# Chunked attention and a feed-forward layer on one core: head pairs scored in row tiles, later operands turned by the DMA crossbar, the front ordered by token tile

## The chip, the core and the metric

The kernel runs on one core of one Trainium2 chip. The metric is device time in microseconds (us), from the start to the end of one execution. The engines are TensorE (PE, matmuls), VectorE (DVE), ScalarE (ACT), GpSimd (POOL) and SyncE (SP, which only issues DMAs here). The kernel before was run three times.

## The reference

Four batches, eight heads, 768 positions, 64 numbers a head, all in float32. Attention is local: the positions go in chunks of 32, and the 32 queries of a chunk see eight memory keys, the chunk itself, 16 positions to its left and 8 to its right.

```python
for c in range(nc):                       # 24 chunks of 32
    k_full = concat(mem_k, k[l_start:r_end])   # 8 + up to 56 keys
    scores = q_c @ k_full.T / sqrt(64)
    a = softmax(scores)                   # 1e-9 is added to the sum
    out[c] = a @ concat(mem_v, v[l_start:r_end])
x = out as (4, 768, 512)
xn = (x - mean(x)) / sqrt(var(x) + 1e-6) * g
result = x + relu(xn @ w_ch1) @ w_ch2     # 512 -> 2048 -> 512
```

## The kernel before

**Tiles and units.** The 3072 tokens are 24 tiles of 128, six a batch. A tile holds two groups of 64 queries, so a batch has twelve groups. The feed-forward part works in units, a list called `units`: tiles 0 to 2 together, then tiles 3, 4 and 5 alone, then six units of three tiles. A unit runs 16 up steps (function `up`, L291: four matmuls each, of 128 columns for every tile of the unit; the ReLU goes to DVE at L299 and to ACT at L297 in turn) and then four down steps a tile (`down`, L308, four matmuls of 512 columns each, then the product with the root of the variance and the sum with x at L315, and the store from SP at L318).

**Attention of a tile** is four functions. `scores` (L212) does, per group and pair of heads, one matmul of 128x128 by 128 columns: the two heads of a pair lie in rows 0 to 63 and 64 to 127, and QZ, the query operand, holds zeros where a head meets the other's keys. Two exponentials on ACT (L219) follow, with a bias column that hides what a chunk must not see. `values` (L231) does 16 matmuls of 65 columns, of which the last column is the count of ones that gives the softmax's sum; DVE takes the reciprocal (L238), multiplies (L239), and takes statistics (L246, L247). The centred token is written at L258 (DVE) or L253 (POOL). `turn_x` (L274) turns it in four PE transposes and DVE copies it out (L279).

**Keys and queries** are loaded by POOL in runs of 512 numbers for a whole batch or two parts of it (`load_kq`), cast to fp16 on the way. `kq_block` turns them on PE (L188) and copies them to KT on DVE (L196) and QZ on ACT (L204). V is loaded in runs of 64 numbers (L106, L112); its left and right borders are copied from neighbour groups by SP (`v_before`, `v_after`), the memory values by `v_mem`.

**Order.** There is no scheduler: every engine runs its instructions in the order in which the Python code issues them. Work beside a unit is put into a dictionary, `plan`, which says after which step it is issued. In the first unit the plan has the scaling of w1 by the gain g (`scale_w1`, L154, 16 instructions on DVE), the clears of the second V buffer (`clear_v`, L334 to L336), its counts (L340) and the clears of KT and QZ (L346 to L349). [...] Two PSUM slots called `att` serve attention, four called `mm` serve the feed-forward part, each in turn.

Of the kernel before, what the change touches and what calls it, by code (L numbers as in the profile page):

```python
# [15 lines left out]
def kernel(  # L16
# [15 lines left out]
    FF = 2048  # L32
    NG = 12
    KR = 104
    BLK = 72
    KC = 24 + NG * BLK + 32
    HD = 65
    CUT = 64
# [6 lines left out]
    memk16 = sb.tile([8, B * H, 64], FP16, name="memk16")  # L45
    memv16 = sb.tile([8, B, H, HD], FP16, name="memv16")
    memKT = sb.tile([128, B * 4, 8], FP16, name="memKT")
    g_col = sb.tile([128, 4], FP32, name="g_col")
    band = sb.tile([128, 2], FP32, name="band")
    zero2 = sb.tile([128, 2], FP32, name="zero2")  # L50
    ones3 = sb.tile([128, 3], FP16, name="ones3")
    hole = sb.tile([128, 1], FP16, name="hole")
# [3 lines left out]
    k16 = [sb.tile([96, H, 8, 64], FP16, name=f"k16_{i}") for i in range(2)]  # L56
    q16 = [sb.tile([96, H, 8, 64], FP16, name=f"q16_{i}") for i in range(2)]
    V = [sb.tile([128, NG, H, HD], FP16, name=f"V{i}") for i in range(2)]
    KT = [sb.tile([128, 4, KC], FP16, name=f"KT{i}") for i in range(2)]
    QZ = [sb.tile([128, 4, NG, 2, 64], FP16, name=f"QZ{i}") for i in range(2)]  # L60
    AT = [sb.tile([128, 2, H, 64], FP16, name=f"AT{i}") for i in range(3)]
    xs = [sb.tile([128, 512], FP32, name=f"xs{i}") for i in range(9)]
    xn = [sb.tile([128, 512], FP16, name=f"xn{i}") for i in range(3)]
    xT = [sb.tile([128, 4, 384], FP16, name=f"xT{i}") for i in range(2)]
    rT = [sb.tile([128, 384], FP16, name=f"rT{hc}") for hc in range(16)]
# [3 lines left out]
    nmean = [sb.tile([128, 1], FP32, name=f"nmean{i}") for i in range(3)]  # L69
# [16 lines left out]
    def free(ap, off, pattern, parts=None):  # L86

        p = list(ap.ap[0]) if parts is None else [ap.ap[0][0], parts]
        return bass.AP(tensor=ap.tensor, offset=ap.offset + off, ap=[p] + [list(x) for x in pattern])
# [3 lines left out]


    HS = S * D

    def load_kq(b, which, lo=0, hi=96):

        dst, src = ((k16, k), (q16, q))[which]
        nc.gpsimd.dma_start(  # L100
            out=dst[b % 2][lo:hi, :, :, :],
            in_=dram(src, b * H * HS + 512 * lo, [[512, hi - lo], [HS, H], [1, 512]]),
        )

    def load_v_group(b, g):
        nc.gpsimd.dma_start(  # L106
            out=V[b % 2][24:88, g, :, 0:64],
            in_=dram(v, b * H * HS + 64 * g * D, [[64, 64], [HS, H], [1, 64]]),
        )

    def load_v_head(b, h):
        nc.gpsimd.dma_start(  # L112
            out=V[b % 2][24:88, :, h, 0:64],
            in_=dram(v, (b * H + h) * HS, [[64, 64], [64 * 64, NG], [1, 64]]),
        )

    def load_v_after(b, g):

        nc.gpsimd.dma_start(
            out=V[b % 2][96:104, g, :, 0:64],  # L120
            in_=dram(v, b * H * HS + 64 * (g + 1) * D, [[64, 8], [HS, H], [1, 64]]),
        )

    def v_before(b, g0, g1):
        vt = V[b % 2]
        nc.sync.dma_start(out=vt[0:16, g0:g1, :, :], in_=vt[72:88, g0 - 1 : g1 - 1, :, :])

    def v_after(b, g0, g1):
        vt = V[b % 2]
        nc.sync.dma_start(out=vt[96:104, g0:g1, :, :], in_=vt[24:32, g0 + 1 : g1 + 1, :, :])  # L130

    def v_mem(b):
        vt = V[b % 2]
        src = memv16[:, b, :, :]
        nc.sync.dma_start(
            out=vt[16:24, :, :, :],
            in_=bass.AP(tensor=src.tensor, offset=src.offset,
                        ap=[list(src.ap[0]), [0, NG], [1, H * HD]]),
# [8 lines left out]

# [3 lines left out]

    def scale_w1(c):
        for dt in range(4):
            nc.vector.tensor_scalar(  # L154
                out=w1c[c][:, dt, :], in0=w1c[c][:, dt, :], scalar1=g_col[:, dt : dt + 1],
# [395 lines left out]
```

The softmax here doesn't subtract the row's maximum and nothing guards it: scores larger than these inputs give would overflow.

## Time and profile before

| | |
|---|---|
| runs | 277.56, 277.69, 278.35 us (median 277.69) |
| profiled execution, its span | 277.4 us |
| busy PE, DVE, ACT, POOL | 231.5, 148.9, 91.1, 80.4 us |
| up matmuls (L291) | 640, 98.6 us |
| down matmuls (L308) | 384, 93.7 us |
| score matmuls (L212) | 192, 16.3 us |
| value matmuls (L231) | 384, 11.7 us |
| transposes of tokens (L274) | 96, 9.9 us |
| transposes of keys and queries (L188) | 384 |
| DMA bytes that arrived | 21.87 MB |
| HBM read, written | 27.43 MB, 6.29 MB |

The page gives one time for the profiled execution, its span from the first to the last instruction; the runs' median is 0.3 us above it. Busy time of PE is that of overlapping matmuls whose ends are modelled, so it is read by windows and by the chain of waits rather than as a share. The slices divide the span into 40 parts of 6.9 us; a digit is a tenth of busy time.

### The profile page before, as it was taken

The page shows a single profiled execution, that of the slowest core. Times are in us where ns is not written, and L with a number is a line of the kernel's source. Part 1 is how long each engine was busy: PE and PEld are TensorE (multiplying, and loading weights), DVE is VectorE, ACT ScalarE, POOL GpSimd, SP SyncE. Part 2 cuts the span into 40 slices and gives each one's busy share as a digit, 9 for nine tenths or more (in the row PEclk, how much of TensorE's full clock was granted, in tenths as well). Part 3 has the DMA queues.
Part 4 walks back from the last instruction along what each step waited for, and adds up shares of the span by engine and source line. Part 5 has one row for each costly group of instructions (what it writes and reads, how often), then busy time and mean ns, then how long its engine had stood idle before and what let it go on. Part 6 is the DMA issues. An engine that isn't in the chain of part 4 may idle for free.

```text
span 277.4 us, 5949 instructions
## 1 busy us (share of the span) xinstructions
PE 231.5 (83%) x2480; PEld 143.3 (52%) x2480; DVE 148.9 (54%) x300; ACT 91.1 (33%) x177; POOL 80.4 (29%) x161
## 2 busy tenths in 40 slices
PE   0255592789919797789999999999999999999993
PEld 0254341345615657357655764666467557646641
DVE  6837658922614754954665555465636446553411
ACT  1074021141300457137344540376234305501300
POOL 6593240000605260370760224053402221320000
PEclk9999999668986999999999999999999999999998
DMA  6999996000694399079979801627950021012002
GB/s 54 146 125 212 213 187 66 0 2 2 80 228 31 73 120 55 2 118 191 67 85 160 182 0 51 94 15 34 95 119 0 2 77 38 4 38 78 0 38 76
DMA packets 40491, 21.87 MB, mean 79 GB/s; under 512 B 28064, under 2 KB 36672, under 8 KB 40416
## 3 DMA queue, kind: packets, MB, share of 16 engines
q0 software_dynamic: 35584, 13.72, 51.4%
q1 hardware_dynamic: 4880, 7.78, 9.8%
q8 instruction: 19, 0.31, 0.4%
q14 instruction: 8, 0.07, 0.1%
HBM read 27.43 MB, written 6.29 MB: 122 GB/s over the span
## 4 chain that ended last, share of the span: by engine, by line
PE 70%; DVE 17%; ACT 4%; DMA 4%; issue 3%; POOL 1%; DVEq 0%; ACTq 0%
PE mm L291 29%; PE mm L308 28%; PE att L188 5%; DMA V<-in_v_dram 4%; DVE V L334 4%; PE att L212 3%; PE att L231 3%; ACT QZ L204 3%; DVE bst L246 2%; DVE xs L239 2%; PE att L274 1%; ACT AT L219 1%; DVE KT L196 1%; DVE osb L315 1%; DVE w1c L154 1%
## 5 line engine op out<-in xcount | busy, mean ns | idle before, releaser
L291 PE MATMUL mm<-xT,w1c 128*128 128x384 f16 (+1 forms) x640 | 98.6, 305 | 11.8 <-DVE w1c L154 7.4
L308 PE MATMUL mm<-w2c,rT 128*128 128x512 f16 x384 | 93.7, 393 | 0.0
L291 PEld LDWEIGHTS <-w1c 128*128 128x128 f16 x640 | 61.3, 116 | 37.8 <-DVE w1c L154 9.0
L297 ACT ACTIVATE rT<-mm 128x384 f16<-128x384 f32 (+1 forms) x80 | 33.5, 427 | 118.1 <-PE mm L291 75.5
L308 PEld LDWEIGHTS <-rT 128*128 128x128 f16 x384 | 36.3, 100 | 40.0 <-issue 5.0
L299 DVE TENSOR_SCALAR rT<-mm 128x384 f16<-128x384 f32 (+1 forms) x80 | 37.3, 471 | 34.1 <-PE mm L291 33.9
L204 ACT COPY QZ<-att 64x512 f16<-64x512 f16 (+2 forms) x48 | 27.8, 579 | 43.9 <-DVE KT L196 43.3
L315 DVE SCALAR_TENSOR_TENSOR osb<-mm,rstd,xs 128x512 f32<-128x512 f32 x24 | 18.0, 750 | 30.5 <-PE mm L308 24.8
L219 ACT ACTIVATE AT<-att,band 104x512 f16<-104x512 f32 x48 | 30.2, 683 | 9.3 <-PE att L212 9.1
L249 POOL TENSOR_SCALAR nmean<-mv 128x1 f32<-128x1 f32 x15 | 2.8, 189 | 87.0 <-DVE mv L247 52.6
L196 DVE COPY KT<-att 128x512 f16<-128x512 f16 (+2 forms) x24 | 16.5, 689 | 16.0 <-PE att L188 13.0
L264 POOL TENSOR_SCALAR veps<-mv 128x1 f32<-128x1 f32 x24 | 6.3, 262 | 59.6 <-DVE mv L247 58.2
L106 POOL DMA_DIRECT2D V<-in_v_dram x24 | 16.6, 697 | 14.0 <-DMA w1c<-in_moe_w_ch_dram 4.6
L212 PE MATMUL att<-QZ,KT 128*128 128x128 f16 x192 | 16.3, 233 | 3.4 <-ACT QZ L204 2.9
L279 DVE COPY xT<-att 128x512 f16<-128x512 f16 x24 | 10.1, 419 | 14.2 <-PE att L274 14.1
L231 PE MATMUL att<-V,AT 104*64 104x65 f16 x384 | 11.7, 206 | 6.6 <-DMA V<-in_v_dram 5.8
L246 DVE BATCH_NORM_STATS2 bst<-xs 128x6 f32<-128x512 f32 x24 | 16.7, 694 | 0.8
L239 DVE TENSOR_TENSOR xs<-att,rec 128x512 f32<-128x512 f32 x24 | 16.6, 691 | 0.8
L212 PEld LDWEIGHTS <-KT 128*128 128x128 f16 x192 | 13.9, 105 | 5.9 <-issue 3.8
L188 PE MATMUL att<-identity,k 64*64 64x64 f16 (+2 forms) x384 | 12.1, 203 | 5.7 <-DMA k<-in_k_dram 2.4
L238 DVE RECIPROCAL rec<-att 128x8 f32<-128x8 f32 x24 | 4.8, 202 | 21.8 <-PE att L231 21.8
L188 PEld LDWEIGHTS <-k 64*64 64x64 f16 (+2 forms) x384 | 10.0, 116 | 12.0 <-issue 6.9
(48 smaller groups left out, 140.1 us busy)
## 6 DMA issues: line engine op xcount, KB each, us to landing
out_dram<-osb SPq DMA_DIRECT2D x24, 256.0 KB
w1c<-in_moe_w_ch_dram POOLq DMA_DIRECT2D x4, 512.0 KB, 8.8
w2c<-in_moe_w_ch_dram POOLq DMA_DIRECT2D x4, 512.0 KB, 15.2
V<-in_v_dram POOLq DMA_DIRECT2D x24, 64.0 KB, 7.4
k<-in_k_dram POOLq DMA_DIRECT2D x2, 768.0 KB, 11.4
q<-in_q_dram POOLq DMA_DIRECT2D x2, 768.0 KB, 14.9
V<-in_v_dram POOLq DMA_DIRECT2D x16, 96.0 KB, 4.5
k<-in_k_dram POOLq DMA_DIRECT2D x2, 512.0 KB, 6.4
```

The lines of the kernel that those rows point to most:

```text
L188: nc.tensor.matmul(out=pv[64 * par : 64 * par + 64, n * r : n * r + n], lhsT=src[b % 2][lo:hi, 2 * j + par, r, :], rhs=identity[lo:hi, lo:hi],
L204: nc.scalar.copy(out=o, in_=i)
L212: nc.tensor.matmul(out=p[:, gg, 128 * j : 128 * j + 128], lhsT=KT[b % 2][:, j, BLK * g : BLK * g + 128], rhs=QZ[b % 2][:, j, g, :, :], sta ...
L219: nc.scalar.activation(out=free(a, 32 * c, [[512, 2], [64, 8], [1, 32]], KR), in_=free(p, 32 * c, [[512, 2], [64, 8], [1, 32]], KR), func= ...
L231: nc.tensor.matmul(out=p[64 * gg : 64 * gg + 64, h // 4, c0 : c0 + HD], lhsT=AT[t % 3][0:KR, gg, h, :], rhs=V[b % 2][0:KR, 2 * t + gg, h, ...
L239: nc.vector.tensor_tensor(out=x.rearrange("p (a h d) -> p a h d", a=2, h=4), in0=free(p, 0, [[512, 2], [HD, 4], [1, 64]]), in1=free(r, 0, ...
L246: nc.vector.bn_stats(out=bst[i], in_=x)
L291: nc.tensor.matmul(out=p, lhsT=free(w, i, [[4, 128]]), rhs=xT[u % 2][:, dt, 0 : 128 * n], start=(dt == 0), stop=(dt == 3),)
L297: nc.scalar.activation(out=o, in_=p, func=ACTF.Relu)
L299: nc.vector.tensor_scalar(out=o, in0=p, scalar1=0.0, scalar2=None, op0=ALU.max)
L308: nc.tensor.matmul(out=p, lhsT=rT[hc][:, 128 * i : 128 * i + 128], rhs=w2c[hc // 4][:, hc % 4, :], start=(hc == 0), stop=(hc == 15),)
L315: nc.vector.scalar_tensor_tensor(out=o, in0=p, scalar=rstd[t % 9], in1=xs[t % 9], op0=ALU.mult, op1=ALU.add,)
```

## The change

Nearly every function is rewritten. The mathematics and the feed-forward weights' layout stay.

- **Scores** are 16 matmuls of 64 columns a tile. The two heads of a pair use rows 0 to 63 and 64 to 127 of the array as separate row tiles and write different PSUM banks. QZ and its zeros are gone.
- **Keys** lie in KT by tile, pair and group in windows of 96: 16 left, 64 own, 8 right, 8 memory. V has the same order and 80 columns a head, 16 of them ones.
- **Batch 0** is loaded, turned on PE and copied tile by tile (`load_tile`, `turn_tile`); V of its first three tiles is loaded with its borders.
- **Batches 1 to 3** are loaded in blocks of 256 positions (`load_block`, two DMAs), reordered by ACT (`mix`, into two buffers in turn), turned by a DMA transpose from SP (`cross`), and for keys spread into KT by DVE (`spread`).
- **Tokens** are multiplied by g where they are centred (`norm`, DVE); w1 is not scaled. From the third unit on (`XU = 2`) a DMA transpose from SP turns them.
- **Units** are eight, of three tiles each. The first one's quarter of w1 is done tile by tile in the front (`up_tile`), the second one's third tile is done in `up_tile` at steps 12 to 15. The last tile's down matmuls are two halves of 256 columns with a store each.
- **Padding**: 28 matmuls on zeros (`warm`) stand in the front.
- Memory keys, memory values and g are loaded by SP; the bias columns and the counts come from sums over the identity matrix on DVE.

```diff
 def scores(b, t):
-            for j in range(4):
-                nc.tensor.matmul(
-                    out=p[:, gg, 128 * j : 128 * j + 128],
-                    lhsT=KT[b % 2][:, j, BLK * g : BLK * g + 128],
-                    rhs=QZ[b % 2][:, j, g, :, :], start=True, stop=True)
+            for j in range(4):
+                for par in range(2):
+                    rows = slice(64 * par, 64 * par + 64)
+                    nc.tensor.matmul(
+                        out=p[0:W, par, (4 * gg + j) * 64 : (4 * gg + j) * 64 + 64],
+                        lhsT=KT[b % 2][rows, t, j, gg, :],
+                        rhs=free(QR[b % 2][rows, t // 2, :, :],
+                                 32 * j + 16 * (t % 2) + 8 * gg, [[128, 8], [1, 8]]),
+                        start=True, stop=True, tile_position=(64 * par, 0))
...
+def load_block(b, blk, which):
+    s = pick(st, ("b", b, blk, which))
+    for par in range(2):
+        nc.gpsimd.dma_start(
+            out=s[:, 512 * par : 512 * par + 512],
+            in_=dram((k, q)[which], (b * H + 4 * par) * HS + blk * 256 * D,
+                     [[HS, 4], [512, 32], [1, 512]]))
+def mix(b, blk, which, eng):
+    s, o = pick(st, ("b", b, blk, which)), pick(iv, ("b", b, blk, which))
+    copy(eng, free(o, 0, [[64, 2], [128, 8], [1, 64]]), s)
+def cross(b, blk, which):
+    i = pick(iv, ("b", b, blk, which))
+    o = QR[b % 2][:, blk, :, :] if which else pick(rawk, ("b", b, blk))
+    nc.sync.dma_start_transpose(out=o, in_=i)
+def spread(b, blk, eng):
+    r, kt, t = pick(rawk, ("b", b, blk)), KT[b % 2], 2 * blk
+    copy(eng, free(kt, 768 * t + 16, [[192, 4], [8, 9], [1, 8]]), ...)
...
+def norm(b, t):
+    i = NT * b + t
+    nc.vector.scalar_tensor_tensor(
+        out=xn[i % 4], in0=xs[i % 9], scalar=mv[t][:, 0:1], in1=gb,
+        op0=ALU.subtract, op1=ALU.mult)
 def turn_x(b, t):
+    if i // 3 >= XU:
+        nc.sync.dma_start_transpose(out=dst, in_=xn[i % 4])
+        return
...
+load_v(0, 0, 16, 88); load_v(0, 1, 0, 88)
+load_tile(0, 1, 1); load_tile(0, 2, 0); load_w1(0)
+load_v(0, 2, 0, 88); load_v(0, 3, 0, 88)
+load_tile(0, 2, 1); load_tile(0, 3, 0)
+load_v(0, 4, 0, 88); load_v(0, 5, 0, 88)
+for c in range(1, 4): load_w1(c)
+load_w2(0); load_tile(0, 4, 0); load_tile(0, 3, 1); load_w2(1)
...
+def attend(i, s0, s1, u):
+    at(u, s0, scores, b, t)
+    at(u, s0, soften, b, t, 0); at(u, s0 + 1, soften, b, t, 1)
+    at(u, s1, values, b, t); at(u, s1 + 1, stats, b, t)
+    at(u, s1 + 2, norm, b, t); at(u, s1 + 2, root, b, t)
+    at(u, s1 + 3, turn_x, b, t)
...
+            attend(6, 14, 17, u); attend(7, 16, 20, u); attend(8, 18, 23, u)
...
+            attend(6 * b, 3, 8, u); attend(6 * b + 1, 8, 14, u)
+            attend(6 * b + 2, 14, 19, u)
+        for i in range(3):
+            attend(6 * b + 3 + i, 1 + 6 * i, 6 + 6 * i, u + 1)
```

Here `at(u, s, f)` issues f after step s of unit u, and a unit has 28 steps. For batch 1 the loads of its six key and query blocks stand at steps 27 of the first unit to 10 of the second, each reordering copy eight steps after its load, the transpose one step after that, and the spreading five steps later. For batches 2 and 3 the loads stand in the third and the fifth unit, with two steps between two loads of keys and queries.

## The prediction

> **What bounds the kernel now.** I read the page's slices first, then a table of windows cut where the units of the feed-forward part begin, then the chain of waits in order of time. The slices:
>
> ```profile
> PE   0255592789919797789999999999999999999993
> PEclk9999999668986999999999999999999999999998
> DMA  6999996000694399079979801627950021012002
> ```
>
> A slice is 6.9 us. TensorE (PE) is full from about slice 17 and has gaps before; its clock falls after the gaps. The DMA engines are full in slices 1 to 5, idle in 7 to 9.
>
> ```profile
> 0.00:31.67 31.67, 11.68 (x228) 9.93 (x229) 21.49 (x40) 9.60 (x15) 19.11 (x43) 1.00 1.06 144
> 31.67:72.90 41.23, 32.92 (x268) 16.93 (x268) 22.55 (x42) 8.12 (x18) 7.61 (x15) 0.83 0.43 60
> ...
> 118.30:150.85 32.55, 31.27 (x456) 19.44 (x454) 18.89 (x37) 15.87 (x29) 14.30 (x25) 1.00 1.21 120
> 150.85:175.13 24.28, 24.28 (x199) 14.68 (x197) 12.61 (x26) 8.29 (x16) 6.43 (x14) 1.00 0.47 95
> 175.13:203.80 28.67, 28.18 (x326) 17.48 (x325) 16.41 (x31) 13.75 (x22) 9.39 (x18) 1.00 0.74 60
> 203.80:228.07 24.27, 24.27 (x198) 14.70 (x197) 12.61 (x26) 7.51 (x14) 4.86 (x12) 1.00 0.12 41
> ...
> 252.35:277.40 25.05, 20.76 (x112) 11.68 (x110) 7.37 (x12) 3.92 (x8) 0.00 (x0) 0.97 0.11 43
> ```
>
> Columns: window, length, busy time of PE, PE's weight load, VectorE (DVE), ScalarE (ACT), GpSimd (POOL), clock, DMA share, GB/s. The last unit is pure feed-forward: 20.76 us of PE for three tiles. A unit that also prepares three tiles of attention takes 24.28, one that turns keys and queries too 28.67 or 32.55; in all of these PE is the bound. In the first 118.3 us six tiles are done, which cost PE 48.6 in the last units' way; PE idles there for 39.8 of the 45.9 us that it idles in all. The chain names the two longest gaps:
>
> ```profile
> 39.76 1.05 DVE w1c L154 x4
> 40.81 1.35 issue
> 42.17 5.26 DVE V L334
> ...
> 72.10 10.75 DMA V<-in_v_dram
> ```
>
> The fill of the second V buffer holds DVE, behind it wait the scaling of w1 and PE (7.2 us idle); later values wait 5.8 us for V of tile 5. A finer table of windows shows the loads:
>
> ```profile
> 12.50:15.00 2.50, 1.06 (x32) 1.05 (x32) 2.25 (x5) 0.83 (x2) 2.42 (x6) 1.00 1.13 81
> 15.00:17.50 2.50, 1.99 (x64) 1.85 (x63) 0.69 (x1) 1.72 (x4) 2.50 (x4) 1.00 1.16 71
> ...
> 22.50:25.00 2.50, 1.59 (x24) 1.26 (x23) 2.30 (x6) 1.40 (x3) 0.62 (x1) 1.00 1.24 210
> ```
>
> V, in runs of 64 numbers, moves at about 76 GB/s (in bytes that arrive), all else at about 210, both with the engines full.
>
> [...] 16 value matmuls take 0.38 us of the chain, 24 ns each. [...] after the 7.2 us gap the trace has 0.50. [...]
>
> **Crossbar price.** [...] A batch has 6x8 + 6x4 = 72 blocks[...]: hidden as a stream, not as latency.
>
> **First group, now 72.9 us up to tile 3's first up matmul.** Loads of batch 0: keys and queries 1.57 MB and weights 4.19 MB at 210 GB/s = 27.5 us; V with its halos 912 rows instead of 776, 0.93 MB at 76 = 12.3 (+1.8). They sum to 39.8, begin near 2.5, lose about 2.5 because V's first load waits for the clears and counts on DVE; the last lands near 47, w2's last part near 44.5. The clears shrink: V's 5.26 + 2x0.49 becomes a fill of 1,536 elements, by the same rate (0.84 ns an element) 1.3 us, and two of 0.3; QZ's 2.7 goes. The 16 scalings of w1 (353 ns) go. Tile order: keys and queries of tile 0 land near 6, V of tile 0 near 11, w1's first quarter near 15. Values, reciprocal, product, statistics and normalisation are 0.65 + 0.2 + 0.69 + 0.69 + 0.18 + 0.75 = 3.2 us a tile, V for tiles 1 and 2 comes near 17 and 21, so tile 2 is turned near 26 and the up matmuls of w1's second quarter start near 27. From there PE needs 48 ups at 0.1625 = 7.8, 48 downs at 0.216 = 10.4, five turns of 16 small matmuls at 25 ns = 2.0, two tiles of attention 2.3: 22.5. End 49.5; V of tiles 3 and 4 is just late, +0.5: 50. The padding matmuls (28) run where PE waits for loads; if that cover went they would cost 0.2 each. The second buffer's fills (about 2.5 us of DVE) fit into the four free PSUM slots (2.6 us of ups); uncovered they cost their own length once.
>
> **Second group, now 72.9 to 118.3 for tiles 3 to 5.** One unit replaces three: 64 ups of 256 columns at 0.109 = 7.0, 64 of 128 at 0.065 (the rate in single-tile units) = 4.2, 48 downs 10.4, attention of four tiles 3.5: 25.1. New waits: each reordering copy for the crossbar stands on ACT (1,024 elements; 512 take 579 ns, 768 take 793, so 1.0 us), waits for its load and, from the third on, for the crossbar to have read the buffer of two before[...]. Behind it stand the ReLUs, behind these PSUM slots and PE. Four copies fall into four steps of 0.44 us: I charge 6 us (0 if the loads are early, 12 if each wait is paid). On DVE the spreading copies (288 + 704 + 320 elements, 1.5 us) wait for the crossbar before a ReLU: in the 6. Tile 8's values come at step 23 of 28; [...] late by about 4.5 us, with the cold clock. End 50 + 25.1 + 6 + 4.5 = 85.6. The SP queue carries V copies, crossbar and output in order; V's copies grow by 80/65, unseen unless one stands before tile 8's turn. POOL issues 24 loads at 0.7 = 17 us here, in time for the V copies.
>
> **Five steady units, now 118.3 to 252.35 = 134.05.** Feed-forward 20.77. Scores: 16 matmuls of 64 columns, two row halves side by side; 16 x 25 ns = 0.40 against 0.445 now. [...] Values 0.38. The turning of tokens (24.28 - 20.77 - 3 x 0.83, a third: 0.34) and of keys and queries leaves PE. Unit 20.77 + 3 x 0.78 = 23.1; DVE has 8 x 0.55 + 3 x 2.5 + 3 x 0.75 + 3 = 17 (0.42 a token copy gone, normalisation now 0.75 with gain, POOL's share moved to it), ACT 3.9 + 4.1 + 3.0 = 11: both below 23. In odd units the third tile's chain ends at about step 24, 3.5 us before the end[...]: I add 3 us over all. 5 x 23.1 + 3 = 118.5. End 204.1.
>
> **Last unit.** 20.8, then half an output product 0.45 instead of 0.75 and a store of half size; 4.3 now, 3.3 then. Sum 50 + 35.6 + 118.5 + 24.1 = 228.2 against the span of 277.4; the median of the runs is 277.69, 0.1% more, so 228 stands for both.
>
> **Rivals.** Hidden better (18%): ACT and DVE find the crossbar done, -6; tile 8 and odd units late by half, -4; row pairs overlap, -3: 216. For it: ACT is idle half of every unit. Against: the fixed two buffers.
> Crossbar slower, still hidden as a stream (16%): 0.5 us a block[...]; four in a row in the second group +8, five unit ends +1.5: 243. For it: unpriced here; odd units have 3.5 us.
> Row tiling does not do what it says (8%): 0.9 a tile, 18 tiles x 0.5 = +9: 237.
> Slower than now (7%): the crossbar as stream becomes the bound. 216 blocks from 52 us on, then a last unit and tail of 21[...]. It decides from (277.4 - 73)/216 = 0.95 us a block. [...]
> Forecast 50%, its own range 220 to 238; 1% is left for no change.
>
> **Numbers.** A difference of 0.3% is about what a measurement here can tell. All cases but two are faster: 0.92; same 0.01; slower 0.07. The range 213 to 246 takes in 216, 237, 243 and the unknown prices but not the slow case.
>
> **What would show it.** Right: tile 3's first up near 50, no fill of V over 2 us, score groups at or under 0.4 us, units of 23 us, PE's weight of the span near 80%. Wrong: the chain naming the SP queue or crossbar over 10%, ACT copies of the crossbar input releasing PE by over 12 us, units above 25, or the first group over 55 because V or w2 lands late.

## The result, and the profile after

The changed kernel takes 311.2 us (median of four runs, 309.76 to 314.44); in the same session the kernel before took 277.62 (277.01 to 278.35). The ratio is 1.1175, 95% interval 1.1112 to 1.1239: 12% slower where 18% faster was forecast. The profiled execution's span is 310.0 us. Ratios here compare undisturbed executions only, so that one can lie a little beside that of the medians.

The slices of the changed kernel, 7.75 us each:

```profile
PE   8477599666547666776849689769885988789995
...
PEclk9756579979685959999998999987977999999999
DMA  7999990007999026599997014979991021002002
```

PE starts earlier than before (in the first slices much of that is the padding on zeros), but then never fills up: digits of 4 to 8 with a few nines run through to the last slices, where before there were nines from slice 17. The table of windows, cut where each unit's first up matmul starts and once more at 24 us (columns as in the prediction: PE, weight load, DVE, ACT, POOL, clock, DMA share, GB/s):

```profile
0.00:24.00 24.00, 15.40 (x177) 7.51 (x177) 10.03 (x36) 13.00 (x10) 16.63 (x28) 0.79 1.35 139
24.00:71.80 47.80, 36.70 (x380) 21.76 (x373) 21.74 (x50) 22.65 (x24) 12.60 (x23) 0.79 0.59 96
71.80:128.00 56.20, 34.39 (x309) 22.29 (x309) 21.88 (x47) 28.58 (x25) 21.23 (x35) 0.79 0.91 102
128.00:161.90 33.90, 24.36 (x209) 13.71 (x210) 17.36 (x34) 23.36 (x20) 18.58 (x30) 1.00 1.32 135
161.90:192.00 30.10, 25.96 (x208) 14.19 (x208) 14.92 (x30) 17.59 (x14) 6.58 (x11) 0.94 0.38 74
...
257.40:285.60 28.20, 24.17 (x209) 13.73 (x208) 13.93 (x26) 17.47 (x14) 2.77 (x6) 1.00 0.15 43
285.60:310.00 24.40, 21.01 (x129) 13.39 (x127) 7.59 (x13) 3.92 (x8) 0.00 (x0) 0.97 0.12 44
```

The first group ends at 71.8 us and not at 50, the second takes 56.2 and not 35.6, and the steady units, forecast at 23.1, take 28.2 to 33.9. Only the last, 24.4, is as forecast. In the unit from 128.0 ACT is as busy as PE (23.36 and 24.36 of 33.9 us); the forecast had ACT at 11. Even 257.4 to 285.6, with DMA nearly idle (0.15), is 5 us longer than forecast. The page's chain of waits, shares of the span by engine and line:

```profile
PE 39%; ACT 28%; DMA 17%; DVE 5%; issue 5%; SPq 3%; POOL 1%; ACTq 0%; DVEq 0%; POOLq 0%
ACT AT L263 24%; PE mm L363 17%; PE mm L337 13%; DMA V<-V 6%; DMA st<-in_k_dram 5%; DMA xT<-xn 4%; PE att L274 3%; DMA QR<-iv 3%; ACT rT L329 2%; PE att L253 2%; PE mm L348 2%; ACT iv L98 2%; SPq L230 1%; DVE osb L372 1%; PE mm L385 1%
```

Before, ACT and DMA were 4% of the chain each; now 28% is ACT, nearly all of it the exponential (L263), and 17% is DMA. The exponential's row in the groups of the profile, before and after (instructions, then busy us, mean ns of one, idle time before):

```profile
L219 ACT ACTIVATE AT<-att,band 104x512 f16<-104x512 f32 x48 | 30.2, 683 | 9.3 <-PE att L212 9.1
```
```profile
L263 ACT ACTIVATE AT<-att,band 96x512 f16<-96x512 f32 x48 | 116.3, 2589 | 11.8 <-PE att L253 11.5
```

One takes 2589 ns, before 683 (48 of each, 104 rows then, 96 now). And pieces of the chain in order of time (start, length, what):

```profile
72.46 8.27 DMA V<-V
...
85.38 7.99 DMA QR<-iv
...
105.24 2.74 ACT AT L263
...
108.83 2.39 ACT AT L263
...
118.73 3.30 DMA V<-V
...
157.38 4.47 DMA xT<-xn
```

Besides exponentials (AT), the chain waits for the border copies of V (V<-V, 8.27 us for a copy inside SBUF), for the crossbar's queries (QR<-iv, 7.99) and for turned tokens (xT<-xn). The 5% for keys from memory (st<-in_k_dram) are the first load, 9.96 us at the start, and one wait of 4.12 us in the third group. So there were three suspects: the exponential, the crossbar and the border copies. A transfer is said to land when its reader may go on. In what follows a stage is named by its unit: units 0 and 1 are the first and second group, units 2 to 6 the steady ones, unit 7 the last. The times from the unit starts of the traces, with the forecast's 3 us for late ends spread over the five steady units:

| us | unit 0 | 1 | 2 | 3 | 4 | 5 | 6 | 7 | span |
|---|---|---|---|---|---|---|---|---|---|
| forecast | 50 | 35.6 | 23.7 | 23.7 | 23.7 | 23.7 | 23.7 | 24.1 | 228.2 |
| the changed kernel | 71.8 | 56.2 | 33.9 | 30.1 | 33.7 | 31.7 | 28.2 | 24.4 | 310.0 |
| exponential rewritten (e1) | 59.4 | 52.2 | 34.6 | 28.0 | 32.6 | 29.9 | 24.1 | 24.4 | 285.2 |
| e1 without later loads (e10) | 59.1 | 49.3 | 24.0 | 29.6 | 24.1 | 30.7 | 24.0 | 24.4 | 265.2 |
| e1, V with its borders (e12) | 59.4 | 45.6 | 40.3 | 25.5 | 37.5 | 26.0 | 24.0 | 24.3 | 282.6 |
| keys, queries by PE, V with borders (e11) | 58.3 | 39.6 | 31.2 | 24.3 | 29.7 | 23.8 | 24.0 | 24.4 | 255.3 |

Keys, queries and V of the next batch are loaded in units 2 and 4, and used from units 3 and 5 on. The last three rows are explained where their runs are. Gaps cost more than their length in units 0 and 1: the mean granted clock of the changed kernel is 0.79 in both, and there up matmuls of 256 columns start 213 ns apart at 81.4 us, where the granted clock is 0.50 after a wait of PE of 5.28 us, and 109 at 71.8 us, where it is 1.00. No run separates this part from the waits that go with it.

### The profile page after: what moved, and what is told of

Read it like the earlier page. It is cut to its first block, busy times and chain, and to the rows that moved or that the text cites. A ratio compares the mean times of both kernels' runs of the same rounds, so it can differ in the third digit from the quotient of the medians.

```text
span 310.0 us, 5080 instructions
## 1 busy us (share of the span) xinstructions
PE 236.5 (76%) x2024; PEld 136.3 (44%) x2024; DVE 140.4 (45%) x301; ACT 167.7 (54%) x148; POOL 98.6 (32%) x164
## 3 DMA queue, kind: packets, MB, share of 16 engines
q1 hardware_dynamic: 33856, 15.43, 25.9%
## 4 chain that ended last, share of the span: by engine, by line
PE 39%; ACT 28%; DMA 17%; DVE 5%; issue 5%; SPq 3%; POOL 1%; ACTq 0%; DVEq 0%; POOLq 0%
ACT AT L263 24%; PE mm L363 17%; PE mm L337 13%; DMA V<-V 6%; DMA st<-in_k_dram 5%; DMA xT<-xn 4%; PE att L274 3%; DMA QR<-iv 3%; ACT rT L329 2%; PE att L253 2%; PE mm L348 2%; ACT iv L98 2%; SPq L230 1%; DVE osb L372 1%; PE mm L385 1%
## 5 line engine op out<-in xcount | busy, mean ns | idle before, releaser
L263 ACT ACTIVATE AT<-att,band 96x512 f16<-96x512 f32 x48 | 116.3, 2589 | 11.8 <-PE att L253 11.5
L329 ACT ACTIVATE rT<-mm 128x384 f16<-128x384 f32 (+2 forms) x66 | 37.1, 580 | 75.8 <-PE mm L337 48.4
L337 PEld LDWEIGHTS <-w1c 128*128 128x128 f16 x496 | 56.3, 119 | 37.8 <-issue 15.5
L331 DVE TENSOR_SCALAR rT<-mm 128x384 f16<-128x384 f32 (+2 forms) x65 | 35.4, 547 | 52.2 <-PE mm L337 47.4
L363 PEld LDWEIGHTS <-rT 128*128 128x128 f16 x368 | 35.6, 101 | 42.3 <-issue 6.0
L274 PE MATMUL att<-V,AT 96*64 96x65 f16 x384 | 12.1, 210 | 37.2 <-ACT AT L263 24.6
L130 POOL DMA_DIRECT2D V<-in_v_dram x48 | 34.8, 729 | 12.2 <-DMA st<-in_k_dram 4.6
L98 ACT COPY iv<-st 128x1024 f16<-128x1024 f16 x18 | 19.9, 1113 | 22.6 <-DMA rawk<-iv 15.0
L372 DVE SCALAR_TENSOR_TENSOR osb<-mm,rstd,xs 128x512 f32<-128x512 f32 x23 | 17.0, 748 | 29.9 <-PE mm L363 28.9
L274 PEld LDWEIGHTS <-AT 96*64 96x64 f16 x384 | 9.2, 122 | 47.2 <-ACT AT L263 31.4
L100 DVE COPY KT<-rawk 128x288 f16<-128x288 f16 (+2 forms) x27 | 14.1, 580 | 13.1 <-DMA rawk<-iv 13.1
L253 PE MATMUL att<-QR,KT 64*96 64x64 f16 x384 | 15.2, 224 | 5.3 <-ACT AT L263 4.1
L296 DVE SCALAR_TENSOR_TENSOR xn<-xs,mv,gb 128x512 f16<-128x512 f32 x24 | 17.9, 747 | 0.5
L253 PEld LDWEIGHTS <-KT 64*96 64x96 f16 x384 | 12.7, 138 | 12.1 <-issue 11.4
L306 POOL TENSOR_TENSOR rstd<-veps,mhalf 128x1 f32<-128x1 f32 x24 | 13.3, 555 | 2.0
## 6 DMA issues: line engine op xcount, KB each, us to landing
st<-in_k_dram POOLq DMA_DIRECT2D x24, 128.0 KB, 6.9
st<-in_q_dram POOLq DMA_DIRECT2D x24, 128.0 KB, 7.5
```

Of the source, the lines that this page charges most:

```text
L98: eng.copy(out=out, in_=in_)
L130: nc.gpsimd.dma_start(out=V[b % 2][lo:hi, g, :, 0:64], in_=dram(v, b * H * HS + (64 * g - 16 + lo) * D, [[64, hi - lo], [HS, H], [1, 64]]),)
L253: nc.tensor.matmul(out=p[0:W, par, (4 * gg + j) * 64 : (4 * gg + j) * 64 + 64], lhsT=KT[b % 2][rows, t, j, gg, :], rhs=free(QR[b % 2][rows ...
L263: nc.scalar.activation(out=free(AT[t % 3], 32 * c, [[64, 16], [1, 8], [8, 4]]), in_=free(p, 4 * c, [[64, 16], [8, 8], [1, 4]], W), func=AC ...
L274: nc.tensor.matmul(out=p[64 * gg : 64 * gg + 64, par, HD * j : HD * j + HD], lhsT=AT[t % 3][:, par, gg, j, :], rhs=V[b % 2][:, 2 * t + gg, ...
L296: nc.vector.scalar_tensor_tensor(out=xn[i % 4], in0=xs[i % 9], scalar=mv[t][:, 0:1], in1=gb, op0=ALU.subtract, op1=ALU.mult,)
```

## The experiments

### The exponential

The changed exponential reads a score row of 64 queries and writes it so that successive numbers lie 8 fp16, 16 bytes, apart, because the queries come out of the crossbar in another order than the values need. Theory: that walk is the price. e1 keeps source, destination and values and only lets the same instruction walk in the order of the destination:

```diff
-            out=free(AT[t % 3], 32 * c, [[64, 16], [1, 8], [8, 4]]),
-            in_=free(p, 4 * c, [[64, 16], [8, 8], [1, 4]], W),
+            out=free(AT[t % 3], 32 * c, [[64, 16], [8, 4], [1, 8]]),
+            in_=free(p, 4 * c, [[64, 16], [1, 4], [8, 8]], W),
```

> The changed kernel with the two inner loops of the exponential exchanged: the same elements to the same places, but the innermost loop is now the eight tokens that lie side by side in the destination (source step 8), instead of four tokens 16 bytes apart. Theory A (the exponential's access pattern makes it 2.59 us instead of 0.68 and ScalarE the bound of every unit): one exponential falls to about 0.7 us, a steady unit to 23 to 26 us, the whole to 235 to 250 us. Theory B (the crossbar and the copies of V on the SP queue end last, the exponentials only fill their shade): the exponential may get shorter, the time stays above 285 us. Theory C (the price lies in reading PSUM at a step, not in the writes): the exponential stays at 2.5 us or more and the time at about 311 us.

```profile
L263 ACT ACTIVATE AT<-att,band 96x512 f16<-96x512 f32 x48 | 31.1, 678 | 14.4 <-PE att L253 14.2
```

678 ns, so theory A has the cause and theory C is out. But the time fell only from 311.2 to 285.1 us (282.03 to 287.48), 1.0145 of the kernel before (1.0102 to 1.0187), far from A's 235 to 250 and at the edge of B. So 26 of the 83 us of error are this one line's walk, and most of the error is something else. By the table they lie in unit 0 (12.4), unit 1 (4.0) and unit 6 (4.1); in units 2 and 4, where something else is late too, the cheaper exponential wins almost nothing.

e2 puts the reordering elsewhere, into PE's read of the queries (the moving operand, the `rhs` of the matmul), with a plain exponential:

```diff
-                                 [[128, 8], [1, 8]]),
+                                 [[1, 8], [128, 8]]),
...
-            out=free(AT[t % 3], 32 * c, [[64, 16], [8, 4], [1, 8]]),
-            in_=free(p, 4 * c, [[64, 16], [1, 4], [8, 8]], W),
+            out=free(AT[t % 3], 32 * c, [[64, 16], [1, 32]]),
+            in_=free(p, 32 * c, [[64, 16], [1, 32]], W),
```

> The changed kernel with the order of tokens made by the score matmul (the moving operand is read at a step of 128 elements, so that the scores leave in the order of tokens) and the exponential on runs of 32 on both sides, as in the kernel before. Theory A: the exponential is at 0.68 us and the time at 235 to 250 us if the stepped read costs TensorE nothing; the score group goes from 0.47 us to 0.9 us or more if it does, which adds 0.45 x 3 = 1.4 us a unit. Theory B: above 285 us.

```profile
L253 PE MATMUL att<-QR,KT 64*96 64x64 f16 x384 | 25.7, 284 | 1.3 <-ACT KT L98 0.7 <-ACT QR L98 0.5
```

The exponential is again 678 ns, but a score matmul, whose moving operand now steps 256 bytes from number to number, takes 284 ns and not the 214 of e1 (25.7 us of busy time and not 13.9). Over 24 tiles that is 1.07 us of busy time for the 16 score matmuls of a tile and not 0.58, as the text had it for a stepped read that is not free. The time is 292.31 us (290.57 to 294.31), 7 us above e1. Of the two, the order is better paid on ACT's read of PSUM, where it costs nothing that shows: 678 ns with the stepped read of e1 and with the plain one of e2.

e3 keeps the changed kernel's read and its short inner loop of four, but writes densely (the numbers of a group then lie in another order than the values take them):

```diff
-            out=free(AT[t % 3], 32 * c, [[64, 16], [1, 8], [8, 4]]),
+            out=free(AT[t % 3], 32 * c, [[64, 16], [4, 8], [1, 4]]),
```

> The changed kernel with the exponential's reads left as they are (runs of four), but written in dense runs of four: the places of tokens within a tile are thereby exchanged, nothing is left out. If the distance between written elements (2 bytes every 16) is the price, one exponential falls to about 0.7 us and the time to 235 to 250 us. If the short inner loop of four is the price, it stays near 2.5 us and the time near 311 us.

It took 679 ns, and the whole kernel 287.24 us in its one execution, again not 235 to 250: the loop's shape and the read add nothing to the 678 ns of e1, the write is the price of the exponential (2589 ns), and the rest of the error lies elsewhere. e4 is the reverse, the kernel before with nothing but this pattern in its exponential (again another order within a group):

```diff
-                out=free(a, 32 * c, [[512, 2], [64, 8], [1, 32]], KR),
-                in_=free(p, 32 * c, [[512, 2], [64, 8], [1, 32]], KR),
+                out=free(a, 32 * c, [[64, 16], [1, 8], [8, 4]], KR),
+                in_=free(p, 4 * c, [[64, 16], [8, 8], [1, 4]], KR),
```

> The kernel before with only the exponential's pattern taken from the changed one (inner loop of four, written 16 bytes apart): the places of scores within a tile are thereby exchanged, the work is the same. Theory A: the exponential goes from 0.683 to about 2.6 us, ScalarE's busy time from 91 to about 183 us; in a unit of 24.3 us ScalarE would have 3.9 + 6 x 2.6 = 19.5 us, so the time rises by what does not fit beside the ReLUs: 20 to 50 us, to 298 to 328 us. Theory B: within 5 us of 277.6.

2624 ns each, 348.46 us, 1.2517 of the kernel before (1.2461 to 1.2573). The pattern alone costs that kernel 70 us, more than the 20 to 50 expected, and more than the 26 it costs the changed one, where by the table units 2 and 4 are held by something else too.

What about the write is dear? e14, e15 and e16 change only the step of the changed kernel's write and leave its read alone (each puts the weights of a group in another order, which leaves the work the same):

```diff
-            out=free(AT[t % 3], 32 * c, [[64, 16], [1, 8], [8, 4]]),
+            out=free(AT[t % 3], 32 * c, [[64, 16], [1, 2], [2, 16]]),    e14
+            out=free(AT[t % 3], 32 * c, [[64, 16], [1, 4], [4, 8]]),     e15
+            out=free(AT[t % 3], 32 * c, [[64, 16], [1, 16], [16, 2]]),   e16
```

> The exponential of the changed kernel with its read as it was; it writes the same 512 numbers a partition with 4 bytes between successive ones (the weights of each group of 32 queries lie in another order, so the sums that follow are of other weights). Line theory (a write is dear when the next one leaves the 16-byte line): near 680 ns, four writes to a line. Distance theory (cost grows with the step, any gap is paid): 900 to 1300 ns.

> As the run before, 8 bytes between successive writes (again in another order within a group of 32 queries). Line theory: two writes to a 16-byte line, 680 to 900 ns. Distance theory: half of the way, 1300 to 1700 ns.

> As the run before, 32 bytes between successive writes (again in another order). Line theory: one write a line as with 16 bytes, 2.6 us. Distance theory: dearer than with 16 bytes, over 3.2 us.

```profile
L263 ACT ACTIVATE AT<-att,band 96x512 f16<-96x512 f32 x48 | 37.3, 819 | 15.2 <-PE att L253 12.4 <-DVE rT L331 2.6
```
```profile
L263 ACT ACTIVATE AT<-att,band 96x512 f16<-96x512 f32 x48 | 62.9, 1397 | 15.3 <-PE att L253 15.2
```
```profile
L263 ACT ACTIVATE AT<-att,band 96x512 f16<-96x512 f32 x48 | 119.6, 2661 | 11.4 <-PE att L253 11.1
```

The whole kernel took 284.17, 286.41 and 315.97 us, one execution each. With e3 (2 bytes) and the changed kernel (16 bytes), which have the same read:

| step of the write | 2 bytes | 4 | 8 | 16 | 32 |
|---|---|---|---|---|---|
| stretches of 16 bytes that 512 writes enter | 64 | 128 | 256 | 512 | 512 |
| one exponential, ns | 679 | 819 | 1397 | 2589 | 2661 |

Neither theory was right as put. Four writes to a stretch of 16 bytes were not free (819 ns against 679) and two took twice the dense price (1397), against the line theory; from 16 to 32 bytes next to nothing more is paid (2589 and 2661), against the distance theory, which had over 3.2 us there. All five fit a price for every stretch of 16 bytes entered: from 128 to 256 stretches 4.5 ns each, from 256 to 512 4.7, above a fixed part that is about 0.24 us by estimate (819 less 128 times 4.5), and never under the 679 ns of the dense write. A price that grows with the step and stops growing at 16 bytes would give the same five numbers; no run separates the two. A line of 16 bytes was the author's supposition: the runs show that the price stops growing at that step, not why.

### The crossbar

In e1 the chain through unit 2 now shows the crossbar plainly (start, length, what):

```profile
124.36 11.02 DMA QR<-iv
...
135.48 1.05 ACT iv L98
...
136.55 9.36 DMA QR<-iv
...
147.09 1.23 SPq L230
...
149.34 0.57 SPq L137
...
150.00 6.13 DMA V<-V
```

A query block lands 11.0 us after it is issued, the reordering copy (`iv`, 1.05 us) that waits for its buffer follows, then the next block in 9.4; at the unit's end stands a border copy of V. What a block costs was the author's estimate in the forecast; no trace of the kernel before shows one. Is the wait for one of the two buffers the cause? e5 gives six and three:

```diff
-    iv = [sb.tile([128, 1024], FP16, name=f"iv{i}") for i in range(2)]
-    rawk = [sb.tile([128, 8, 128], FP16, name=f"rawk{i}") for i in range(2)]
+    iv = [sb.tile([128, 1024], FP16, name=f"iv{i}") for i in range(6)]
+    rawk = [sb.tile([128, 8, 128], FP16, name=f"rawk{i}") for i in range(3)]
```

> As the kernel with the exponential in runs of eight (283 us), with six buffers instead of two ahead of the crossbar and three instead of two behind it, so that ScalarE's reordering copy never waits for a transpose to have read its buffer. Theory A2 (ScalarE and the ReLUs behind it stand because of that wait: 10.4, 9.4, 10.5, 8.1 us in the chain): the third and fifth unit fall from 34.6 and 32.6 to 25 to 27 us, the whole to 262 to 270. Theory B2 (the transposes themselves come late, and VectorE's spreading copies and the next scores wait for them instead): no more than 5 us are won, 278 to 284.

```profile
DVE KT L100 <- DMA rawk<-iv: 30.8, 6, 7.7
```

284.24 us (283.28 to 285.19): nothing won, as theory B2 has it. ACT's 37.3 us of waiting for a buffer in e1 are gone. In their place DVE's spreading of the keys waits 30.8 us for the crossbar (22.8 in e1), with a longest of 7.7, and ACT's copies wait 13.5 us for the keys' loads from memory (4.8 in e1). So two buffers are not the bound: what they wait for is late in itself.

e6 takes the tokens off the crossbar and turns them on PE, as before:

```diff
-    XU = 2
+    XU = 8
```

> As the kernel with the exponential in runs of eight (283 us), with all tokens turned on TensorE and copied by VectorE, as in the first two units. It adds 18 x 0.34 = 6 us of TensorE and takes 18 of the 36 transposes from the SP queue. If the waits for turned tokens at the ends of units (19.4 us of TensorE waiting) are real cost: 268 to 276 us. If they only hide other waits: 283 to 290.

```profile
PE att L319 <- DVE xn L296: 23.2, 18, 6.6
```

298.11 us (297.95 to 298.26), 13 more than e1: PE's instructions run in the order of the code, and it now waits 23.2 us at the token transposes (L319) for DVE's normalised token, in place of a wait of 19.4 at the up matmuls. So the waits at the ends of units were not to be had for nothing, and the crossbar for tokens is a gain, of 13 us in this version.

e7 is e1 with the loads of V for batches 2 and 3 left out (old values are used):

```diff
-                order.append((load_v, (b, g), s))
+                if b == 1:
+                    order.append((load_v, (b, g), s))
```

> As the kernel with the exponential in runs of eight, with V of batches 2 and 3 not loaded (their values use what the buffers hold from batches 0 and 1): the third and fifth unit then have only the loads of keys and queries beside the crossbar. If the transposes are slow because V's many small packets share the 16 DMA engines: a transpose of a key or query block lands within 3 to 5 us, these units fall to 24 to 27 us and the whole to about 265. If a transpose is slow by itself: it still takes 8 us or more and the units stay above 30 us.

283.02 us (280.5 to 285.53). Units 2 and 4 came to 30.5 and 29.0, still far from 24, and the first query block of unit 2, whose loads are now of keys and queries alone, even took 12.7 us; a later one, from 140.7 us on, 3.2. So neither theory holds whole: V's many small packets are not the cause by themselves, and a transfer is not slow by itself. None of the 18 issues of a block on SP took over 3.0 us in e7 (median 1.3), less than a quarter of the 12.7: the landing can be late without a long issue. e10 leaves out all loads of keys, queries and V for batches 2 and 3, and keeps everything that is done with them:

```diff
+                    if b == 1:
-                    order.append((load_block, (b, blk, which), s))
+                        order.append((load_block, (b, blk, which), s))
...
+                if b == 1:
-                order.append((load_v, (b, g), s))
+                    order.append((load_v, (b, g), s))
```

> As e1, but the loads of keys, queries and values of batches 2 and 3 are left out (their tiles work on what the buffers still hold); reordering copies, crossbar transfers, V copies, token and output transfers stay. Theory (the crossbar transfer is late only because loads share the DMA engines with it): from unit 3 on key and query blocks land in 3.3 to 4.4 us after issue, units 4 and 5 take 24 to 26 us, the time is 262 to 272 us. Rival (the transfer is slow by itself when several follow each other, or the SP queue holds it): still 7 to 11 us a block in units 4 and 5, units of 29 us or more, time above 278 us.

```profile
108.40:132.40 24.00, 23.99 (x208) 13.74 (x209) 17.08 (x34) 13.29 (x20) 4.00 (x8) 1.00 0.51 93
132.40:162.00 29.60, 25.52 (x209) 14.29 (x208) 15.36 (x31) 7.83 (x15) 3.33 (x6) 0.94 0.40 76
162.00:186.10 24.10, 24.10 (x210) 13.80 (x209) 16.67 (x34) 13.32 (x20) 4.38 (x8) 1.00 0.43 95
186.10:216.80 30.70, 26.11 (x210) 14.83 (x209) 15.46 (x31) 7.68 (x14) 3.33 (x6) 0.89 0.40 70
```

267.06 us, in one execution. Units 2 and 4 (the first and third line) fall from 34.6 and 32.6 us to 24.0 and 24.1 with PE full: six crossbar blocks a unit with their copies and spreading are hidden, as forecast. The block issued at 125.06 on SP lets ACT go on at 128.20, the next, issued at 127.04, at 131.50:

```profile
125.06 1.26 SPq L230 DMA_TRANSPOSE rawk<-iv  x1
...
127.04 1.29 SPq L230 DMA_TRANSPOSE QR<-iv  x1
```
```profile
128.20 1.04 ACT L98 COPY iv<-st 128x1024 f16<-128x1024 f16 x1 [3.72 <-DMA rawk<-iv]
131.50 1.04 ACT L98 COPY iv<-st 128x1024 f16<-128x1024 f16 x1 [2.25 <-DMA QR<-iv]
```

3.1 and 4.5 us from issue to use. What the forecast missed is how late a block lands while POOL's loads are in flight: 11.0 and 9.4 us in unit 2 of e1. The rival, that the copies wait for late loads and not for the crossbar, does not hold: of the waits of the reordering copies in e1 37.3 us end with a crossbar transfer and 4.8 with a load of keys, and the chain through unit 2 has two of the first kind and none of the second. Units 3 and 5 stay at 29.6 and 30.7; they have another cause.

e8 removes the crossbar altogether, for e6's tokens and for the keys and queries of batches 1 to 3, which are loaded and turned by `load_tile` and `turn_tile` as in batch 0:

```diff
-    order = batch(1, 27, 1, 1, (((0, 1), range(6)), ((2,), range(6, 12))))
-    later(1, order, 0)
+    later(1, tiles_by_pe(1, 27, 2, 9), 0)
...
-        order = batch(b, 0, 2, 1, [((i,), range(4 * i, 4 * i + 4)) for i in range(3)])
-        later(b, order, 2 * b - 2)
+        later(b, tiles_by_pe(b, 0, 3, 9), 2 * b - 2)
```

> As the kernel with the exponential in runs of eight, without any crossbar transpose: tokens of all units and keys and queries of all batches are turned on TensorE tile by tile, as batch 0 is in the changed kernel. TensorE gets 18 x 0.34 + 36 x 0.37 = 19.4 us more. Theory B (latency of the crossbar in the SP queue, not bandwidth or the schedule, makes the units with loads long): third to sixth unit 26 to 28 us each, the second 36 to 42, the whole 250 to 262 us. Theory D (the loads of the next batch are late whatever turns them): the third and fifth unit stay above 30 us, the whole above 272.

273.89 us (273.05 to 276.14), 0.9876 of the kernel before (0.979 to 0.9962): about 1% under it, the first that is, and 24 us under e6. By its numbers theory D holds: units 2 and 4 take 31.0 and 31.1 us and the whole is above 272. Its cause does not: PE waits for loads of keys and queries for 2.9 us in the whole of e8, and its longest wait of any kind is 3.3 us, for a border copy of V. e9 is e8 with the tokens on the crossbar again (`XU = 2`):

> Rewritten exponential writes as in e1; keys and queries are turned on TensorE as in e8, token tiles by the crossbar as in the changed kernel. Theory (the late landing of the key and query blocks, and in e8 the wait of TensorE, in order, for the normalised tokens, are two separate costs): the units of the second and later groups come to 25 to 28 us, the time to 250 to 258 us. Rival (the token tile's crossbar lands as late under loads as the key blocks did, so nothing is won over e8): 270 to 276 us, with up matmuls waiting for XT.

268.44 us (267.02 to 272.27), 0.9626 (0.9548 to 0.9703), between theory and rival and outside of both: 5 us were won and not 16 or more. In e8 PE's wait at the token transposes (L319) had been 7.9 us, no longer the 23.2 of e6, so less was there to be won; and the rival's wait for turned tokens did not come, 2.9 us in all. 9.9 us stand at the values, for V's border copies, as in e8 (9.2).

### The border copies of V

Where in units 3 and 5 is the time? The chain of e10 at the start of unit 5:

```profile
188.07 1.18 SPq L230
...
189.30 0.76 SPq L145
...
190.12 0.56 SPq L137
...
190.72 6.42 DMA V<-V
...
197.27 0.65 PE att L274 x16
```

On the SP queue stand, in order, a crossbar transfer (L230), the memory values (L145), the left borders of V (L137), the right ones: and the values of the unit's first tile (L274) wait until 197.1. Ahead of them in the same queue are the output stores of the unit before, 256 KB each. The copy itself moves 220 KB within SBUF, and takes 6.42 us to land in a unit with no loads at all. That the stores ahead of it are the reason was not tried. The forecast had set this aside ("unseen unless one stands before tile 8's turn"): it stands at the start of the unit, where there is nothing to hide it. e11 is e9 with every 64 positions of V loaded with their borders, so that there are no such copies, for 88 rows of V in place of 64:

```diff
-                order.append((load_v, (b, g), s + 1))
+                order.append((load_v, (b, g, 16 if g == 0 else 0, 80 if g == NG - 1 else 88), s + 1))
...
-            at(u, 0, v_left, b, 1, 12)
-            at(u, 0, v_right, b, 0, 11)
```

> As e9, but each 64-token group of V is loaded with its borders from memory, so that no border copies go through the SP queue behind output stores. Theory (those copies, 6 to 10 us behind the stores, are the wait of the values at the starts of units 1, 3 and 5): 6 to 12 us less than e9 in the same call. Rival (V is late because its own loads are late; a third more V bytes makes it later): equal to e9 or up to 8 us more.

```profile
129.10:153.40 24.30, 23.97 (x209) 13.82 (x207) 13.99 (x27) 7.64 (x14) 6.95 (x12) 1.00 0.27 55
153.40:183.10 29.70, 29.54 (x400) 17.12 (x401) 16.79 (x42) 13.73 (x26) 17.66 (x27) 1.00 1.24 131
183.10:206.90 23.80, 23.80 (x210) 13.90 (x209) 13.75 (x26) 7.64 (x14) 3.33 (x6) 1.00 0.27 56
```

256.49 us (254.47 to 258.26), 0.9203 of the kernel before (0.9138 to 0.9268): 12 us less than e9, and 8% faster than the kernel this began with. Units 3 and 5 are at 24.3 and 23.8 us (first and third line). PE is busy for 29.54 of unit 4's 29.7 us: what is left there is work, the turning of a batch's keys and queries.

Does the same help the crossbar version? e12 makes e11's edit to V in e1:

> As e1 (keys, queries and tokens turned by the crossbar), but each 64-token group of V is loaded with its borders, so that the border copies behind the output stores are gone. Theory (two separate costs: the border copies about 12 to 20 us in all, and landings of 7 to 11 us of key and query blocks under loads, which stay): 265 to 273 us, units 3 and 5 near 24 us, units 2 and 4 still at 31 to 35. Rival (copies and landings are one cost, the queue that both share: without the copies the blocks land early too): 250 to 256 us, units 2 and 4 under 27 us.

It took 282.88 us (279.69 to 284.98), 1.0113 of the kernel before (1.0074 to 1.0151), so within 3 us of e1: neither theory. The table's row tells why. Units 1, 3 and 5 won 6.6, 2.5 and 3.9 us, as the first theory has it; but units 2 and 4 lost 5.7 and 4.9, for there the crossbar lands later still. The chain at the end of unit 4:

```profile
183.69 8.32 DMA QR<-iv
...
193.19 5.16 SPq L230
...
198.44 9.85 DMA xT<-xn
...
208.33 1.75 PE mm L337 x5
```

A query block lands after 8.32 us; SP then spends 5.16 us to issue another (1.3 the median of such issues in e10); only behind it can the token tile be issued, which lands after 9.85, and PE waits for it: 30.8 us in four such waits. In e11, where no blocks are in the queue, the longest wait for a token tile is 3.9. So the costs are two, but in this version they do not add: with the border copies gone and V's loads a third larger, ACT's copies wait 47.1 us for buffers (37.3 in e1) and DVE's spreading 32.5 for the crossbar (22.8). That the larger loads are the reason fits e10, but no run of this version leaves them out.

### The first group

In all variants with the cheap exponential unit 0 ends at 58 to 61 us and not at 50. e13 is e11 without the 28 padding matmuls (all `warm` calls removed):

> As e11, without the 28 matmuls on zeros that keep TensorE busy while the first loads come. Theory (they lie on the chain of the first group, at half clock, and make up half of its 8 us over the forecast): first unit ends at 53 to 56 us instead of 58.3, 2 to 5 us less than e11. Rival (they only fill waits for loads, and without them the clock is halved longer): 0 to 5 us more than e11.

257.57 us (255.48 to 258.5), unit 0 at 59.4: no difference that can be told, so the theory is out. The padding does change PE's pace: the 16 up matmuls of the third tile take 1.87 us without it and 1.05 with it. The mean granted clock of the execution does not show that, 0.986 without it and 0.959 with it. The slower pace is as the rival has it, but PE waits there anyway (2.84 us for DVE's normalised token just before), and the 1.1 us that unit 0 is longer are not clear of noise. What the chain of e11 shows instead:

```profile
5.53 7.05 DMA st<-in_q_dram
12.62 0.64 PE att L203 x16
...
32.62 0.67 PE mm L337 x4
...
34.13 1.35 DVE V L527
...
37.32 4.06 PE mm L337 x24
```

Queries of the first tile let PE go on at 12.6 us (the forecast had them near 6): landing alone takes 7.05. The second quarter's up matmuls start at 32.5 and not at 27. The fill of the second V buffer (1.35 us, its size as forecast) stands ahead of a ReLU on DVE, but 24 of the 48 up matmuls are done before PE has to wait for it, 0.79 us. From 32.5 to 58.3 are 25.8 us, of which PE is busy for 23.5, against 22.5 and 0.5 of waits in the forecast. So 5.5 of the 8.3 us are the late start, 1 is work, and the rest waits, the longest of 1.31 us at the end, for DVE's normalised token.

## Why the prediction was wrong

The step that failed first is ScalarE's sum: it took an exponential at 0.683 us, and the changed one takes 2.589. Two more terms were set far too low: the crossbar's landing beside loads, and the border copies of V, at nothing. The sum was 50 + 35.6 + 118.5 + 24.1 = 228.2; the trace has 71.8 + 56.2 + 157.6 + 24.4 = 310.0. By step:

- **"ACT 3.9 + 4.1 + 3.0 = 11: below 23."** This term failed most plainly. 4.1 is six exponentials at the old 0.683 us; the diff changes their access pattern, and the text gave that no price, not even a bound. At 2.589 they take 15.5, ACT 22.4 a unit, as long as PE. Cost: 26 us, shown by e1 and, in reverse, by e4. No rival held it. (The 3.0 for reordering copies is a mean, too: the loading units 2 and 4 have all six of a batch, 6 us, and the others none.)
- **"Hidden as a stream, not as latency."** The stream was small, as forecast. Packets of SP's queue took 10.5% of 272.2 us in e8, 16.2% of 265.7 in e9, 25.9% of 310.0 in the changed kernel: by difference 0.20 us a block for 72 blocks of tokens, 0.24 for all 216 (0.29 in e1), so 17 us for the 72 blocks of a batch. Alone a block was there after 3.1 to 4.5 us (e10). But the latency, the author's estimate, which no trace then showed, was set without the loads, and the blocks stand beside the loads of the next batch: 8.0 us in the second group of the changed kernel, 11.0 and 9.4 in unit 2 of e1 with a DMA share of 1.44, up to 13.7 in e12. Without those loads 18 us go (e10 against e1; 20 by the spans, 19 of these in units 2 and 4); the second group, where batch 1 is loaded, has another part that was not separated.
- **"V's copies grow by 80/65, unseen unless one stands before tile 8's turn."** Failed: a landing of 6 us stands at the start of units 3 and 5, and one in unit 1. Without them 4.0, 4.4 and 2.5 us go there; between e9 and e11 it is 12 by the medians.
- **First group, 50.** 58.3 in e11: the first loads start the up matmuls 5.5 us late. The term that failed is "keys and queries of tile 0 land near 6"; the queries let PE go on at 12.6. The fill was nearly covered, 0.79 us.
- **Second group, 35.6.** In the changed kernel 56.2. The exponential is 4.0 of that, the border copies, forecast at nothing, 6.6 (e12 against e1), the crossbar for keys and queries another 6.0 (e11 against e12). The last is net: e11 turns batch 1's keys and queries on PE instead, 12 times 0.37 us by its chain, so the waits charged at 6 come to some 10 by this estimate. 39.6 are left in e11. The 4.5 for tile 8 was not separated.
- **Scores at 0.40.** The 16 of a tile take 0.47 us in the chain, the 8 before took 0.445: row tiling in pairs won nothing, and the rival's sign (slower) was right with a seventh of its size (0.07 us a tile over the forecast, not 0.5). The rival's 0.9 a tile is near what e2's stepped operand takes, 1.07 us of busy time where e1 has 0.58.
- **Right:** the steady unit when nothing holds it (24.0 to 24.1 for 23.1, so 0.9 short), the last unit and tail (24.4 for 24.1), the sizes of the clears, the tokens' crossbar as a gain.

The parts can't be added up to the whole error, since no run joins all cures. The nearest is e11, whose span of 255.3 us is 27.1 above the forecast: 8.3 in the first group, 4.0 in the second, 13.5 in units 2 and 4, where PE turns the keys and queries that the forecast had left to the crossbar, and 1.3 in the rest.

The rival that ended on the slow side took the crossbar as a bound of the stream at over 0.95 us a block. The kernel did get slower, but not so: at 0.24 a block the stream is far from it. Of the marks set for a wrong forecast, units above 25 us came true, and the first group was over 55, though by the exponential and not by V or w2. The mark of 10% of the chain for the SP queue or the crossbar came true only in the wide reading: crossbar landings are 7% (QR<-iv 3%, xT<-xn 4%), SP's issuing 3% and the border copies, which stand in the same queue, 6%. In e1, with the exponential out of the way, crossbar landings are 16% (14% and 2%).

What stays open: by which mechanism the loads delay a crossbar transfer. The records show both a later landing and, with more loads, a longer issue on SP (1.3 us in e10, up to 5.2 in e12). The long issue is not needed for the late landing (at most 3.0 us for an issue in e7, 12.7 for a landing), but whether both have one root was not tried. Nor was it tried to place the border copies ahead of the stores, or on another queue.

## What to carry to other kernels

When a rewrite changes the access pattern of an instruction, price that instruction again even if its shape and count stay: here one walk over the same 512 numbers cost 26 us, and walking in the order of the destination gave it back at no price that shows. A transfer's latency is to be taken from a stretch with the traffic that will run beside it (here 3.1 to 4.5 us without loads and 8.0 to 13.7 beside them), and every wait is to be sought at the place where its reader stands with nothing to do, which for a batch's operands is the start of the unit. When two delays share a queue or the DMA engines, undo both before judging either: the border copies were worth 12 us in one version and 2 in another.

## What the hardware showed that was not expected

- An exponential of ScalarE that writes fp16 to SBUF took 679, 819, 1397, 2589 and 2661 ns for 512 numbers a partition at steps of 2, 4, 8, 16 and 32 bytes (e3, e14, e15, the changed kernel, e16). A stepped read of PSUM by the same instruction added nothing (678 in e1, 678 with the plain read of e2).
- A moving operand of 64 columns that steps 256 bytes took 284 ns a score matmul (e2) and not 214 (e1), and 16 of them 1.07 us of busy time and not 0.58.
- A crossbar transfer of 256 KB (SBUF to SBUF) was there after 3.1 to 4.5 us without loads (e10) and after 8.0 to 12.7 beside them (the changed kernel, e1, e7), up to 13.7 in e12; SP's issue of one took 1.3 us in e10 (median) and up to 5.2 in e12.
- A copy of 220 KB within SBUF, queued behind output stores, landed after 6.4 us with no loads in flight (e10).
- Without the padding (e13) the 16 up matmuls of the third tile took 1.87 us from 31.3 us on, with it (e11) 1.05 us from 31.6 us on, although the mean granted clock of the execution was 0.986 without it and 0.959 with it.
